# Second batch's keys moved behind the start of the MLP, key sums in four quarters of TensorE, and the last output in two halves

## The chip, the core and the metric

The program runs on one core of a Trainium2 chip. The metric is the device time of one execution in microseconds, as a median of several runs. The engines are TensorE (PE in the profile, its weight loads PEld), VectorE (DVE), ScalarE (ACT), GpSimd (POOL) and SyncE (SP), whose queue issues all DMAs before the change.

## The reference

The program computes a linear attention with a quadratic feature map, and behind it a gated MLP on the attention's output. There are 4 batches, 4 heads, 1088 positions, head size 32, and r = 8.

```python
def phi(x):
    a = np.einsum('rd,bhsd->bhsr', S1, x)
    b = np.einsum('rd,bhsd->bhsr', S2, x)
    return np.einsum('bhsi,bhsj->bhsij', a, b).reshape(*x.shape[:-1], r * r)
q_p, k_p = (phi(q), phi(k))
kv = np.einsum('bhsf,bhsd->bhfd', k_p, v)
z = np.sum(k_p, axis=2)
num = np.einsum('bhsf,bhfd->bhsd', q_p, kv)
den = np.einsum('bhsf,bhf->bhs', q_p, z)[..., None] + 1e-06
attn = num / den
# x = attn as 4352 tokens x 128
xn = x / sqrt(mean(x * x) + 1e-06) * rms_g
g, val = xn @ w_gate, xn @ w_val           # 128 -> 1536
out = (g / (1 + exp(-g)) * val) @ w_out    # 1536 -> 128
```

z is a sum over positions of products a_i b_j. It is therefore the diagonal blocks (one per head) of A^T B, where A holds the 32 columns a of the four heads and B the 32 columns b.

## The kernel before

The 4352 tokens are worked through in chunks of 512 (the ninth has 256). A **slot** is one block of 128 of the 1536 hidden units for one chunk: three MLP products into `g_ps`, three into `v_ps` (L822: each fp32 operand is split in a high and a low fp32r part), a Silu on ACT (L829), a product h on DVE (L833), a split of h (ACT L242; DVE L250 or POOL L249), and three products into `o_ps` (L853), or one plain fp32 product in the first 12 and the last 2 slots (L840). The first two chunks take hidden blocks 0 to 5 first (`CUT`), then blocks 6 to 11; the others take 12 slots in a row. In the first two slots the products are made in halves of 256 tokens (`HEAD`).

The weights arrive as 64-bit words (L383) and are turned into fp32 in five steps (`to_f32`: ACT or DVE L330/L306, then DVE L310, L315, L320, L324), and then split (`split`: ACT L242, POOL L249), 384 columns a hidden block.

Ahead of the MLP's first slot stands the **head** of the program: the keys of batch 0 (`kside(0)`: products with S in L482, the outer product phi on DVE or POOL in L501, kv and z in L531), the queries of chunk 0 (`qphi`: L572, L581, turned in L591), numerator and denominator (`nmm`, L659), the division (DVE L722, L723, L715), the mean square (L729, L739), its root on POOL (L757), the normalised x (L760, L780), its turn on TensorE (L764) and the split in `x_hi` (ACT L787) and `x_lo` (DVE L767). For chunk 0 the division and all after it are done in two halves of 256 tokens.

The keys of batches 1 to 3 go through `kside` and `kv_turned`: `mms` makes 18 products of 64x64 (L482), ACT copies the results (L509), DVE multiplies (L501). In `kvmm` nine products of all 64 columns (a and b of four heads) with the 32 columns b (L401) make a Gram matrix whose blocks hold z, and 36 products (L407) make kv in the four column quarters of the array, one head each. `turn` (L430, L433) spreads and turns the results into `kvs[b]`.

The order of work is written by a planner (`Plan.run`). Each task has a key (the slot by which it is due), a duration in ns for each engine it may run on, and buffers; the planner simulates the engines with these durations and picks tasks by key. Every engine then runs its instructions strictly in the planned order. Where TensorE would idle before 20 us, the planner puts in filler products on zeros (`keep_warm`, L292). The last constants that bear on the change: `K1` are the keys of batch 1's steps and of its loads, `AHEAD` gives batch 1's keys two of the three `att` buffers right behind chunk 0's numerators, `SBD` names batches whose phi is computed from the SBUF copy alone, and `DLAT` is the planner's DMA latency.

Of the kernel before, what the change touches and what calls it, by code (L numbers as in the profile page):

```python
# [10 lines left out]
F32 = mybir.dt.float32  # L11
# [9 lines left out]
R = 8  # L21
# [53 lines left out]
K1 = -41,9,10,-26.5  # L75
SBD = (1,)
AB2 = (-21, -20, -19)
# [3 lines left out]
AHEAD = 1  # L81
DLAT = 2400
# [30 lines left out]
class Plan:  # L113
# [49 lines left out]
    def run(self, clock, filler, slow, urgent, window):  # L163
        clock, todo, out, port, form = dict(clock), self.tasks, [], 0, False
        while todo:
# [33 lines left out]
            t.on, t.end = e, at + ns + (DLAT if e == "dma" else 0)  # L199
# [10 lines left out]
def attention_then_glu(ctx, tc, kT, v, qT, sw, w, gain, out):  # L210
# [25 lines left out]
    def load(nbytes, key, emit, writes, reads=()):  # L236
        plan.add({"dma": (nbytes / 320, emit, 0)}, key, reads, writes)
# [23 lines left out]
    spread = const.tile([NB, H, F], F32, name="spread")  # L261
    for h in range(H):
        nc.vector.tensor_copy(
            out=spread[:, h].rearrange("p (i j) -> p i j", j=R),
            in_=ident[:NB, 2 * h * R:(2 * h + 1) * R].unsqueeze(2).to_broadcast([NB, R, R]),
        )
    column = const.tile([P, R], F32, name="column")
    nc.vector.tensor_reduce(out=column, in_=ident.rearrange("p (o j) -> p j o", j=R), axis=AX.X, op=ALU.add)
# [95 lines left out]
    load(-400 * 320, -99, lambda: nc.sync.dma_start(out=s_raw.rearrange("p n c -> p (n c)"), in_=sw.bitcast(U32)), ["s_raw"])  # L364
# [25 lines left out]
    abs_of, ahead = {}, {}  # L390

    def kv_turned(b, kv, vt, phis, abs_, key):
        acc, tr = ps("att", 3), ps("att", 3)
        both, gram, picked = sb("kv_both", [P, 2, F], 1), sb("gram", [NB, H * R], 1), sb("picked", [P, 2, R], 1)

        def kvmm():
            for t in range(KT):
                ab = abs_[t // 3]()[:, t % 3]  # L400
                nc.tensor.matmul(  # L401
                    out=tr()[:NB, :H * R], lhsT=ab.rearrange("p h c r -> p (h c r)"), rhs=ab[:, :, 1, :], start=(t == 0), stop=(t == KT - 1)
                )
# [9 lines left out]
            1450, key, kvmm, [(phis[g], g) for g in range(3)] + [(vt, g) for g in range(3)] + [(abs_[g], g) for g in range(3)],  # L413
            [acc, tr], True,
        )
        act(H * R, key, lambda: nc.scalar.copy(out=gram(), in_=tr()[:NB, :H * R]), [tr], [gram])
# [10 lines left out]
        def turn():  # L427
            for h in range(H):
# [9 lines left out]
                out=picked(), in0=sums(), in1=column.unsqueeze(1).to_broadcast([P, 2, R]), op=ALU.mult  # L438
# [18 lines left out]
    def kside(b, keys, early):  # L457
# [34 lines left out]
        for i, (lo, hi) in enumerate(groups):  # L492
# [15 lines left out]
            def bring(ab=ab, ab_ps=ab_ps, ts=ts, m=m, o=o, c0=int(first and near)):  # L508
                nc.scalar.copy(  # L509
                    out=ab()[:, ts].rearrange("p t h c r -> p (t h) c r")[:, :, c0:],  # L510
                    in_=ab_ps()[:, o:o + m * HALF].rearrange("p (th c r) -> p th c r", c=2, r=R)[:, :, c0:],
                )
# [4 lines left out]
            if near or b in SBD:  # L517
                dve(m * 268, kphi, lambda outer=outer: outer(nc.vector), [(ab, i), ab_ps] if near else [(ab, i)], [(phi, i)], b in SBD)
# [6 lines left out]
        for i, (lo, hi) in enumerate(groups):  # L525
# [10 lines left out]
            pe(275 * (hi - lo), key, kvmm, [(phis[i], i), (vt, piece[i])], [acc], True)  # L536
# [10 lines left out]
    xs, phiqs = {}, {}  # L547
# [134 lines left out]
    def qside(c, keys, also=None):  # L682
# [9 lines left out]
        if first and AHEAD:  # L692

            ahead[1] = [ps("att", 3) for _ in range(2)]
            if AHEAD > 1:
                abs_of[2] = ps("att", 3)
# [269 lines left out]
```

## Time and profile before

| what | value |
|---|---|
| median of 3 runs | 270.78 us (270.42 to 270.82) |
| the profiled execution's own time | 270.91 us |
| its span, first to last instruction | 269.1 us |
| PE busy | 262.6 us, 98% of the span |
| DVE busy | 189.5 us, 70% |
| ACT busy | 153.2 us, 57% |
| POOL busy | 66.7 us, 25% |
| first MLP product (L822) begins | 19.46 us |
| last output DMA is issued | 266.43 us |

How to read it: the share of busy time is an average over the head, the long MLP stretch and the tail. The granted TensorE clock is shown apart; half of it doubles the time of a product. In the view of the chain of waits, "issue" is time in which an engine waited for nothing that the profile shows. One fp32 product is recorded as two instructions, so 18 products are shown as x36.

### The profile page before, as it was taken

What the parts mean: (1) busy time and instruction counts of PE and PEld (TensorE: products, weight loads), DVE (VectorE), ACT (ScalarE), POOL (GpSimd) and SP (SyncE); (2) the same over time, 40 slices, a digit from 0 to 9 for tenths busy, and PEclk for the clock granted to TensorE, in tenths of its full rate; (3) what the DMA queues carried; (4) which work ended last, traced back from release to release, by engine and by line L of the source; (5) the groups of instructions that cost most, each with busy time, mean ns of one, the idle gap of its engine ahead of it and who ended that gap; (6) DMA issues with size and microseconds to landing.
All of it is one profiled execution on the core that took longest, in us unless ns stands there. A gap on an engine that the chain in (4) does not pass through costs nothing.

```text
span 269.1 us, 5080 instructions
## 1 busy us (share of the span) xinstructions
PE 262.6 (98%) x1899; PEld 208.9 (78%) x1899; DVE 189.5 (70%) x378; ACT 153.2 (57%) x319; POOL 66.7 (25%) x79
## 2 busy tenths in 40 slices
PE   8889999999999999999999999999999999999995
PEld 5758677677887878878887887788887888788894
DVE  5769999666847887677666795678568566766532
ACT  4457763675654544565556554565655565665662
POOL 3033751367350130001800220003300700100262
PEclk9979999999999999999999999999999999999999
DMA  6999500642521520035002500024002200100010
GB/s 202 363 388 371 181 2 0 200 110 58 130 67 48 153 57 2 1 100 131 26 0 80 148 11 2 0 85 130 4 0 68 61 0 0 40 2 0 0 41 21
DMA packets 12953, 22.11 MB, mean 82 GB/s; under 512 B 1664, under 2 KB 5760, under 8 KB 12928
## 3 DMA queue, kind: packets, MB, share of 16 engines
q1 hardware_dynamic: 12928, 21.78, 25.8%
q8 instruction: 15, 0.25, 0.4%
q14 instruction: 10, 0.08, 0.1%
HBM read 18.69 MB, written 3.08 MB: 81 GB/s over the span
## 4 chain that ended last, share of the span: by engine, by line
PE 96%; DMA 2%; issue 1%; SPq 0%; DVE 0%; ACT 0%
PE g_ps L822 27%; PE v_ps L822 27%; PE o_ps L853 23%; PE o_ps L840 4%; PE att L659 4%; DMA q<-qT 2%; PE att L764 2%; PE att L482 2%; PE att L401 1%; PE att L407 1%; PE att L675 1%; PE o_ps L531 1%; PE att L572 1%; PE att L292 1%; PE att L591 0%
## 5 line engine op out<-in xcount | busy, mean ns | idle before, releaser
L833 DVE TENSOR_TENSOR h<-v_ps,s 128x512 f32<-128x512 f32 (+2 forms) x109 | 71.1, 654 | 28.1 <-PE v_ps L822 12.1
L242 ACT CAST h_hi<-h 128x512 fp32r<-128x512 f32 (+1 forms) x91 | 54.2, 596 | 52.5 <-DVE h L833 52.3
L829 ACT ACTIVATE s<-g_ps 128x512 f32<-128x512 f32 (+1 forms) x108 | 62.0, 574 | 25.1 <-PE g_ps L822 22.5
L250 DVE TENSOR_TENSOR h_lo<-h,h_hi 128x512 fp32r<-128x512 f32 x74 | 53.0, 720 | 32.0 <-ACT h_hi L242 31.0
L822 PE MATMUL g_ps<-x_hi,w_hi 128*128 128x512 f32 (+1 forms) x110 | 46.0, 419 | 0.0
L822 PE MATMUL v_ps<-x_hi,w_hi 128*128 128x512 f32 (+1 forms) x110 | 42.2, 383 | 0.0
L822 PE MATMUL g_ps<-x_hi,w_lo 128*128 128x512 f32 (+1 forms) x110 | 42.0, 382 | 0.0
L822 PE MATMUL g_ps<-x_lo,w_hi 128*128 128x512 f32 (+1 forms) x110 | 41.7, 379 | 0.0
L822 PE MATMUL v_ps<-x_hi,w_lo 128*128 128x512 f32 (+1 forms) x110 | 41.5, 377 | 0.0
L822 PE MATMUL v_ps<-x_lo,w_hi 128*128 128x512 f32 (+1 forms) x110 | 41.4, 377 | 0.0
L757 POOL TENSOR_TENSOR rstd<-ms,mhalf 128x4 f32<-128x4 f32 (+1 forms) x10 | 9.5, 951 | 112.3 <-DVE ms L773 111.9
L853 PE MATMUL o_ps<-h_hi,w_lo 128*128 128x512 f32 (+1 forms) x94 | 36.1, 384 | 0.0
L853 PE MATMUL o_ps<-h_hi,w_hi 128*128 128x512 f32 (+1 forms) x94 | 36.1, 384 | 0.0
L853 PE MATMUL o_ps<-h_lo,w_hi 128*128 128x512 f32 (+1 forms) x94 | 36.0, 383 | 0.0
L249 POOL TENSOR_TENSOR h_lo<-h,h_hi 128x512 fp32r<-128x512 f32 (+1 forms) x20 | 20.4, 1029 | 30.7 <-ACT h_hi L242 30.6
L822 PEld LDWEIGHTS g_ps<-x_hi,w_hi 128*128 128x128 f32 x110 | 20.7, 188 | 6.5 <-issue 1.8
L822 PEld LDWEIGHTS g_ps<-x_hi,w_lo 128*128 128x128 f32 x110 | 20.7, 188 | 5.0 <-issue 1.7
L822 PEld LDWEIGHTS v_ps<-x_hi,w_hi 128*128 128x128 f32 x110 | 20.7, 188 | 4.6 <-DVE ms L773 0.2
L249 POOL TENSOR_TENSOR w_lo<-w_f,w_hi 128x256 fp32r<-128x256 f32 (+1 forms) x24 | 17.2, 734 | 28.2 <-ACT w_hi L242 28.1
L822 PEld LDWEIGHTS g_ps<-x_lo,w_hi 128*128 128x128 f32 x110 | 20.9, 190 | 4.2
L822 PEld LDWEIGHTS v_ps<-x_hi,w_lo 128*128 128x128 f32 x110 | 20.7, 188 | 4.1 <-issue 0.2
L822 PEld LDWEIGHTS v_ps<-x_lo,w_hi 128*128 128x128 f32 x110 | 20.6, 188 | 4.0
(104 smaller groups left out, 301.3 us busy)
## 6 DMA issues: line engine op xcount, KB each, us to landing
w_raw<-w SPq DMA_DIRECT2D x12, 384.0 KB
at<-far SPq DMA_DIRECT2D x12, 256.0 KB
bt<-far SPq DMA_DIRECT2D x24, 128.0 KB
q<-qT SPq DMA_DIRECT2D x8, 256.0 KB
outT<-o_sb SPq DMA_DIRECT2D x8, 256.0 KB
vt<-v SPq DMA_DIRECT2D x9, 204.0 KB
kt<-kT SPq DMA_DIRECT2D x9, 192.0 KB
far<-abt SPq DMA_DIRECT2D x12, 64.0 KB
```

The source lines that it names most:

```text
L242: "act": (n * 0.835 + 172, lambda: nc.scalar.copy(out=out(), in_=in_()), 0),
L249: "pool": (n * 2.1 + 150, lambda: nc.gpsimd.tensor_tensor(out=out(), in0=in_(), in1=hi(), op=ALU.subtract), 0),
L250: "dve": (n * 1.04 + 140, lambda: nc.vector.tensor_tensor(out=out(), in0=in_(), in1=hi(), op=ALU.subtract), penalty, True),
L482: nc.tensor.matmul(out=abv[hf * HALF:(hf + 1) * HALF, t - t0, :], lhsT=kt()[:, s0:s0 + HALF], rhs=sblk_t, start=True, stop=True)
L659: nc.tensor.matmul(out=nv[hf * HALF:(hf + 1) * HALF, t, p, :], lhsT=phiqs[c][1]()[:, p, l0:l0 + HALF], rhs=kvs[(STARTS[c] + l0) // S][:, p ...
L757: nc.gpsimd.tensor_tensor(out=rstd()[:, us, 0], in0=ms()[:, us], in1=mhalf[:, us], op=ALU.pow)
L764: nc.tensor.transpose(out=xt()[:, t * P:(t + 1) * P], in_=xn()[:, t, :], identity=ident)
L822: nc.tensor.matmul(out=acc()[:, cs], lhsT=wt[:, j, i3, :], rhs=x()[:, cs], start=(i == 0), stop=(i == 2))
L829: act(n, t + 0.3, lambda: nc.scalar.activation(out=s()[:, :n], in_=gps()[:, :n], func=AF.Silu), cols(gps, whole[0]), [s])
L833: lambda cs=cs: nc.vector.tensor_tensor(out=h()[:, cs], in0=vps()[:, cs], in1=s()[:, cs], op=ALU.mult),
L840: lambda cs=cs: nc.tensor.matmul(out=o_ps()[:, cs], lhsT=w_f[:, j, 2], rhs=h()[:, cs], start=first, stop=last and cs.stop == n),
L853: nc.tensor.matmul(out=o_ps()[:, :n], lhsT=wt[:, j, 2, :], rhs=x()[:, :n], start=first and i == 0, stop=last and i == 2,)
```

## The change

It has three named parts and some constants of the planner.

1. **z in four quarters.** In `kvmm` product t no longer multiplies 64 columns by 32, but the 32 columns a by the 32 columns b, and writes into rows 32 (t mod 4) to 32 (t mod 4) + 31 of the same bank; so each column quarter of the array gets two or three of the nine products. The Gram matrix then has 128 rows (four partial sums), `gram` is 128x32, and `spread` has 128 rows, so that L430's products add the quarters. The copy `ab` is laid out so that the 32 columns a are adjacent. `spread` and `column` are now made by POOL (`patterns`, six instructions) where DVE had made them with five.
2. **Batch 1's keys.** `K1` changes, `AHEAD` and `SBD` go: the 18 products L482 of batch 1 stand behind chunk 1's turn and no longer between chunk 0's numerators and its turn. Their phi reads one operand from PSUM, as batches 2 and 3 do.
3. **Last output.** The last chunk's two halves of 128 columns go to two tiles of their own (`o_end0` by ACT, `o_end1` by DVE), and each has a DMA of its own, on ACT's queue and on SP's.

The planner's DMA rate goes from 320 to 340 bytes a ns, its DMA latency from 2400 to 1900 ns, POOL's start from 2200 to 5200 ns, and three durations of TensorE tasks are lowered. The keys of chunk 2's first query steps return to the general rule.

```diff
-K1 = -41,9,10,-26.5
-SBD = (1,)
-AB2 = (-21, -20, -19)
+K1 = (8, 9, 10, -9)
-AHEAD = 1
-DLAT = 2400
...
-        plan.add({"dma": (nbytes / 320, emit, 0)}, key, reads, writes)
+        plan.add({"dma": (nbytes / 340, emit, 0)}, key, reads, writes)
...
+    spread = const.tile([P, H, F], F32, name="spread")
+    column = const.tile([P, 4 * R], F32, name="column")
+    def patterns():
+        nc.gpsimd.tensor_tensor(out=column, in0=ident[:, :4 * R], in1=ident[:, 4 * R:8 * R], op=ALU.add)
+        for k in (2, 3):
+            nc.gpsimd.tensor_tensor(out=column, in0=column, in1=ident[:, 4 * k * R:4 * (k + 1) * R], op=ALU.add)
+        nc.gpsimd.tensor_copy(
+            out=spread.rearrange("p h (i j) -> p (h i) j", j=R), in_=column.unsqueeze(2).to_broadcast([P, H * R, R])
+        )
+        for k in (2, 1):
+            nc.gpsimd.tensor_tensor(out=column[:, :k * R], in0=column[:, :k * R], in1=column[:, k * R:2 * k * R], op=ALU.add)
...
         def kvmm():
             for t in range(KT):
-                ab = abs_[t // 3]()[:, t % 3]
-                nc.tensor.matmul(
-                    out=tr()[:NB, :H * R], lhsT=ab.rearrange("p h c r -> p (h c r)"), rhs=ab[:, :, 1, :], start=(t == 0), stop=(t == KT - 1)
-                )
+                a, b = (abs_[t // 3]()[:, c, t % 3].rearrange("p h r -> p (h r)") for c in range(2))
+                rows = slice(t % 4 * H * R, (t % 4 + 1) * H * R)
+                nc.tensor.matmul(out=tr()[rows, :H * R], lhsT=a, rhs=b, start=(t < 4), stop=(t >= KT - 4), skip_group_check=True)
...
-            near = i not in FAR if first else b in NEAR and b not in SBD
+            near = i not in FAR if first else b in NEAR
...
+        if not left:
+            for i, cs in enumerate(rest_of):
+                o_end, wd = sb(f"o_end{i}", [P, P], 1), cs.stop - cs.start
+                if i:
+                    dve(wd * 1.04, t + 1.0, lambda cs=cs, o=o_end: nc.vector.tensor_copy(out=o(), in_=o_ps()[:, cs]), done, [o_end])
+                else:
+                    act(wd, t + 1.0, lambda cs=cs, o=o_end: nc.scalar.copy(out=o(), in_=o_ps()[:, cs]), done, [o_end])
+                load(
+                    wd * P * 4, t, lambda cs=cs, o=o_end, on=nc.sync if i else nc.scalar: on.dma_start(
+                        out=out[:, s0 + cs.start:s0 + cs.stop], in_=o()
+                    ), [("out", c, i)], [o_end],
+                )
+            return
...
-    plan.run({"pe": PE0, "act": 1900, "dve": 1000, "pool": 2200, "dma": 600}, keep_warm, SLOW, URGENT, WINDOW)
+    plan.run({"pe": PE0, "act": 1900, "dve": 1000, "pool": 5200, "dma": 600}, keep_warm, SLOW, URGENT, WINDOW)
```

The planner's new order shows at three places. First TensorE between chunk 0's numerators and the first MLP products, before (L659 are the numerators, L482 batch 1's keys, L292 filler, L764 the turn of one half of x, L572 chunk 1's queries, L822 the MLP):

```order
L659 MATMUL att<-kv_82,phiq 64x66 x16
L482 MATMUL att<-s_t,kt 64x64 x18
L292 MATMUL att<-const-float32-0.0 1x128 x2
L764 MATMUL att<-ident,xn 128x128 x2
L292 MATMUL att<-const-float32-0.0 1x128 x2
L764 MATMUL att<-ident,xn 128x128 x2
L572 MATMUL att<-s_t,q 128x64 x2
L822 MATMUL g_ps<-x_hi,w_hi 128x256
```

And now (L295 is filler, L757 the turn, L815 the MLP):

```order
L659 MATMUL att<-kv_83,phiq 64x66 x16
L295 MATMUL att<-const-float32-0.0 1x128 x9
L757 MATMUL att<-ident,xn 128x128 x2
L295 MATMUL att<-const-float32-0.0 1x128 x2
L815 MATMUL g_ps<-x_hi,w_hi 128x256
L815 MATMUL g_ps<-x_hi,w_lo 128x256
L815 MATMUL g_ps<-x_lo,w_hi 128x256
L815 MATMUL v_ps<-x_hi,w_hi 128x256
L815 MATMUL v_ps<-x_hi,w_lo 128x256
L815 MATMUL v_ps<-x_lo,w_hi 128x256
```

Nine fillers stand where the keys stood, and nine half-width MLP products (the six shown and three more into `g_ps`) now go ahead of the second turn and of chunk 1's queries.

Second DVE from the first query outer product of chunk 0 (`phn`) to the first division, before:

```order
L581 TENSOR_TENSOR phn<-att,abq 128x512 x2
L605 COPY phiq<-g_ps 128x2x256
L310 TENSOR_SCALAR w_tmp<-w_tmp 128x384
L540 COPY kv_82<-o_ps 64x2x33
L315 TENSOR_SCALAR w_tmp<-w_tmp 128x384
L320 SCALAR_TENSOR_TENSOR w_tmp<-w_raw,w_tmp 128x384
L324 SCALAR_TENSOR_TENSOR w_f<-w_raw,w_tmp 128x384
L722 TENSOR_SCALAR den<-att 128x8
L723 RECIPROCAL rden<-den 128x8
L715 TENSOR_TENSOR x<-att,rden 128x256
```

And now:

```order
L581 TENSOR_TENSOR phn<-att,abq 128x512 x2
L313 TENSOR_SCALAR w_tmp<-w_tmp 128x384
L318 TENSOR_SCALAR w_tmp<-w_tmp 128x384
L323 SCALAR_TENSOR_TENSOR w_tmp<-w_raw,w_tmp 128x384
L327 SCALAR_TENSOR_TENSOR w_f<-w_raw,w_tmp 128x384
L309 TENSOR_SCALAR w_tmp<-w_raw 128x384
L313 TENSOR_SCALAR w_tmp<-w_tmp 128x384
L715 TENSOR_SCALAR den<-att 128x8
L716 RECIPROCAL rden<-den 128x8
L708 TENSOR_TENSOR x<-att,rden 128x256
```

The copies of `phiq` and `kv` left DVE (both are ACT's now), and two steps of the second hidden block's weights (L309, L313) came in ahead of the division.

Third TensorE at the start of chunk 1's MLP, before (L840 is the plain fp32 product into `o_ps`, L764 the turn of chunk 1's x):

```order
L840 MATMUL o_ps<-h,w_f 128x512 x3
L764 MATMUL att<-ident,xn 128x128 x4
L822 MATMUL g_ps<-x_hi,w_hi 128x512
L822 MATMUL g_ps<-x_hi,w_lo 128x512
L822 MATMUL g_ps<-x_lo,w_hi 128x512
L822 MATMUL v_ps<-x_hi,w_hi 128x512
```

And now (L833 is that product, L757 the turn):

```order
L833 MATMUL o_ps<-h,w_f 128x512 x2
L757 MATMUL att<-ident,xn 128x128 x4
L833 MATMUL o_ps<-h,w_f 128x512
L482 MATMUL att<-s_t,kt 64x64 x18
L815 MATMUL g_ps<-x_hi,w_hi 128x512
L815 MATMUL g_ps<-x_hi,w_lo 128x512
L815 MATMUL g_ps<-x_lo,w_hi 128x512
```

Batch 1's 18 products stand behind chunk 1's turn. Chunk 0's sixth hidden block, which followed the turn before, is made ahead of it now. Everywhere behind this place TensorE has the same products as before in nearly the same order, the Gram products with 32 columns in place of 64.

More of the change, by code (lines that the diff above doesn't have):

```diff
@@ L259, in attention_then_glu @@
     nc.vector.memset(ones, 1.0)
[L261 to L265, printed above, removed]
-        )
-    column = const.tile([P, R], F32, name="column")
-    nc.vector.tensor_reduce(out=column, in_=ident.rearrange("p (o j) -> p j o", j=R), axis=AX.X, op=ALU.add)
+    spread = const.tile([P, H, F], F32, name="spread")
[6 more added lines that the diff above has]
+            out=spread.rearrange("p h (i j) -> p (h i) j", j=R), in_=column.unsqueeze(2).to_broadcast([P, H * R, R])
+        )
+        for k in (2, 1):
+            nc.gpsimd.tensor_tensor(out=column[:, :k * R], in0=column[:, :k * R], in1=column[:, k * R:2 * k * R], op=ALU.add)
+    patterns()
     zeros = nc.const_aps.tensor(0.0, [P, P], F32)
@@ L412, in kv_turned @@
         pe(
-            1450, key, kvmm, [(phis[g], g) for g in range(3)] + [(vt, g) for g in range(3)] + [(abs_[g], g) for g in range(3)],
+            1330, key, kvmm, [(phis[g], g) for g in range(3)] + [(vt, g) for g in range(3)] + [(abs_[g], g) for g in range(3)],
             [acc, tr], True,
         )
-        act(H * R, key, lambda: nc.scalar.copy(out=gram(), in_=tr()[:NB, :H * R]), [tr], [gram])
+        act(H * R, key, lambda: nc.scalar.copy(out=gram(), in_=tr()[:, :H * R]), [tr], [gram])
         act(
@@ L437, in kv_turned @@
             17, key, lambda: nc.vector.tensor_tensor(
-                out=picked(), in0=sums(), in1=column.unsqueeze(1).to_broadcast([P, 2, R]), op=ALU.mult
+                out=picked(), in0=sums(), in1=column[:, :R].unsqueeze(1).to_broadcast([P, 2, R]), op=ALU.mult
             ), [tr], [picked],
@@ L472, in kside @@
         piece = [next(g for g, (_, e) in enumerate(pieces) if hi <= e) for _, hi in groups]
-        abs_ = [sb("ab", [P, 3, H, 2, R], 3) for _ in groups]
+        abs_ = [sb("ab", [P, 2, 3, H, R], 3) for _ in groups]
         phis = [sb("phi", [P, 3, H * F], 4) for _ in groups]
-        banks = [ps(("g_ps", "v_ps")[i % 2], 2) for i in range(4)] if first else ahead[b] if b in ahead else [ps("att", 3) for _ in range(2)]
+        banks = [ps(("g_ps", "v_ps")[i % 2], 2) for i in range(4)] if first else [ps("att", 3) for _ in range(2)]
         def mm(lo, hi, ab_ps, t0):
@@ L667, in abmm @@
         q, m = phiqs[c][0], CHUNKS[c] // 2
-        if c not in abs_of:
-            abs_of[c] = ps("att", 3)
-        ab_ps = abs_of[c]
+        ab_ps = abs_of[c] = ps("att", 3)
         def emit():
@@ L691, in qside @@
         nums = {u: ps("att", 3) for u in range(0, nt, 2)}
[L692 to L696, printed above, removed]
         if c >= NATURAL:
@@ L873, in slot @@
         else:
-            for i, cs in enumerate(rest_of):
-                if i:
-                    dve(
-                        (cs.stop - cs.start) * 1.04, t + 1.0,
-                        lambda cs=cs: nc.vector.tensor_copy(out=o_sb()[:, cs], in_=o_ps()[:, cs]), done, cols(o_sb, cs),
-                    )
-                else:
-                    act(cs.stop - cs.start, t + 1.0, lambda cs=cs: nc.scalar.copy(out=o_sb()[:, cs], in_=o_ps()[:, cs]), done, cols(o_sb, cs))
+            act(n, t + 1.0, lambda: nc.scalar.copy(out=o_sb()[:, :n], in_=o_ps()[:, :n]), done, cols(o_sb, whole[0]))
         load(n * P * 4, t, lambda: nc.sync.dma_start(out=out[:, s0:s0 + n], in_=o_sb()[:, :n]), [("out", c)], cols(o_sb, whole[0]))
```

27 lines of the change are left out of this document (13 added, 14 removed).

## The prediction

> **What bounds the kernel now.** I read the page first: busy shares and the chain that ended last.
>
> ```profile
> span 269.1 us, 5080 instructions
> PE 262.6 (98%) x1899; PEld 208.9 (78%) x1899; DVE 189.5 (70%) x378; ACT 153.2 (57%) x319; POOL 66.7 (25%) x79
> PE 96%; DMA 2%; issue 1%; SPq 0%; DVE 0%; ACT 0%
> ```
>
> TensorE is the bound, in share and in chain. Then its waits over the whole span (line, releaser, total us, times, longest):
>
> ```profile
> PE att L482 <- issue: 1.2, 1, 1.2
> PE att L292 <- PEq L959: 0.8, 1, 0.8
> PE att L572 <- DMA q<-qT: 0.6, 1, 0.6
> PE att L482 <- PE att L482: 0.6, 1, 0.6
> ```
>
> There are four waits of note, and all belong to the head. Two stand before or in batch 1's keys. From the first MLP product to the last, TensorE waits for nobody, so there a product added or removed counts in full. Only the head and the tail have slack. The chain of waits in order of time shows the head (start, us, what):
>
> ```profile
> 11.39 1.35 PE att L659 x32
> 12.74 1.17 issue
> 13.92 0.93 PE att L482 x24
> ...
> 16.13 0.94 PE att L292 x4
> 17.07 0.62 PE att L764 x2
> 19.65 0.41 PE g_ps L822 x3
> 23.64 0.59 PE att L591 x4
> ```
>
> Behind chunk 0's numerators TensorE has idle time; batch 1's 18 products (36 records) fill part of it. They cost the stream nothing there, but they and the two fillers behind them end at 17.07, and only then does the first turn of x (L764) get its place. The other engines show that x was ready sooner:
>
> ```profile
> 9.22 0.56 ACT L330 ACTIVATE w_tmp<-w_raw 128x384 f32<-128x384 f32 x1 [1.14 <-DMA w_raw<-w]
> 10.59 0.35 DVE L310 TENSOR_SCALAR w_tmp<-w_tmp 128x384 f32<-128x384 f32 x1
> 12.36 0.56 DVE L324 SCALAR_TENSOR_TENSOR w_f<-w_raw,w_tmp 128x384 uint32<-128x384 uint32 x1
> 12.95 0.17 DVE L722 TENSOR_SCALAR den<-att 128x8 f32<-128x8 f32 x1
> 15.49 0.42 DVE L760 TENSOR_TENSOR xn<-x,rstd 128x256 f32<-128x256 f32 x1
> 17.73 0.47 ACT L787 ACTIVATE x_hi<-att,gain_t 128x256 fp32r<-128x256 f32 x1 [1.06 <-PE att L764]
> 18.10 0.68 ACT L780 ACTIVATE xn<-x,rstd 128x128 f32<-128x128 f32 x2
> 18.24 0.48 DVE L767 SCALAR_TENSOR_TENSOR x_lo<-att,gain_t,x_hi 128x256 fp32r<-128x256 f32 x1 [1.75 <-ACT x_hi L787]
> 19.82 0.41 ACT L242 CAST w_hi<-w_f 128x256 fp32r<-128x256 f32 x1
> 22.83 0.68 DVE L581 TENSOR_TENSOR phn<-att,abq 128x512 f32<-128x512 f32 x1
> ```
>
> The first normalised half was finished at 15.91 and lay for 1.1 us; DVE idled 1.75 us for the result of its turn. Last the clock, in stretches cut where the granted clock changes (us, busy PE, PEld, DVE, ACT, POOL, then PEclk):
>
> ```profile
> 5.42:8.83 3.41, 2.84 (x64) 2.64 (x66) 3.25 (x5) 1.14 (x5) 1.07 (x1) 1.00 0.95 330
> 12.24:15.66 3.42, 1.66 (x49) 1.44 (x47) 3.18 (x14) 1.68 (x7) 1.44 (x2) 1.00 1.03 386
> 15.66:19.07 3.41, 3.41 (x23) 1.67 (x19) 1.50 (x5) 2.07 (x9) 1.17 (x2) 0.50 1.02 384
> ```
>
> A stretch in which TensorE was busy 1.66 of 3.42 us is followed by one at half clock; one with 2.84 of 3.41 is not.
>
> **Part 1, z in quarters.** Batch 1's sums and kv in the chain:
>
> ```profile
> 44.31 1.17 PE att L401 x18
> 45.47 1.14 PE att L407 x72
> ```
>
> Nine Gram products (18 records) take 1.17 us, 65 ns a record, though they stream only 32 columns. The 36 kv products in four quarters take 1.14/72 = 16 ns a record, a quarter of that, though they stream 64. So a record costs some 65 ns on its own strip of the array, and four strips run side by side. The new Gram products have the kv products' form: 32 columns of weights, four quarters in turn, one bank. By that row they take 18 x 16 ns = 0.29 us and save 0.88 us; three batches save 2.64 us. Nothing covers these products, so the saving is whole. Bounds: the 18 keys products of another batch, in two halves (first row below), take 1.20/36 = 33 ns a record, which would be 0.60 us and 1.7 us saved in all; with no overlap nothing is saved. A loss is excluded: the weights have half the columns, the moving side is the same. I take the kv row, the nearest in every respect.
>
> The Trainium skill, "TensorE: Matmul & The Clock Gate", section "Wait — 56ns, not 53.3ns?", says that matmuls never start closer than about 25 ns, however small. By it 18 records would need 0.45 us, the three batches would save 2.15 us, and the sum below would be an estimated 0.5 us smaller. The kv row, 16 ns, goes under that floor, so the measurement decides here.
>
> The gram copy on ACT and the spread products (L430) keep their column counts; their 128 rows for 64 cost nothing that is counted by columns. `spread` and `column` go to POOL at the start. POOL's next work there stands in this row:
>
> ```profile
> 5.80 1.07 POOL L501 TENSOR_TENSOR phi<-ab 128x512 f32<-128x512 f32 x1 [3.89 <-ACT ab L509]
> ```
>
> It idled 3.89 us before it. Six small instructions, none over the 1.07 us of this 128x512 one and most a sixteenth of its size, fit in: 0, at worst 0.3 us if they slow DVE's first conversion.
>
> **Part 2, the keys.** What 18 such products cost inside the stream is seen at batch 2:
>
> ```profile
> 94.77 1.20 PE att L482 x36
> 95.97 0.89 PE g_ps L822 x3
> 96.86 0.70 PE v_ps L822 x3
> ```
>
> 1.20 us, and the next three MLP products take 0.89 where three take 0.70: 1.39 us added. On DVE the three outer products stay behind chunk 1's turn, where they were; the three ACT copies come in there, under a TensorE that has its products queued. Between the turn of chunk 1 and its first product there are now one `o_ps` product and these keys, which cover `x_hi` and `x_lo`; with no cover there would be a wait.
>
> Against this stands the head. DVE begins the first weights when ACT's step ends (9.22 + 0.56 = 9.78), no longer waits for the copy of `phiq`, and has six steps ahead of the division: four of 0.35 and two of 0.56, so den comes at about 12.35 where it stood at 12.95. The second weights' data must have landed by 11.6 for that; before, ACT took them at 11.9 only because it was busy. xn stood 2.54 us behind den and lasted 0.42: 15.3 for its end. Nine fillers (0.94/4 = 0.24 us a record at half clock, half that at full: 2.1 us in all) are done by 14.9. So the turn goes at 15.35, not 17.07. `x_hi` follows at 15.8 to 16.3; DVE does two steps of 0.56 first, then `x_lo` until 16.95. MLP products begin at 16.3, in earnest at 16.95, where they began at 19.65.
>
> That is not yet the gain, for the second turn and chunk 1's queries now fall behind this start. I compare at L591 before 23.64, ahead of which the same products stand, now with one more block of three, 0.70 plus some 0.1. It waits for DVE's second `phn`. DVE from 16.95: 1.82 for a weights block (until 18.8), `x_lo` of the second half (whose ACT chain ends at 19.0: 16.3 + 0.41 + 0.56 + 0.68, a turn of 0.4, `x_hi` with a cast 0.65) until 19.5, then `phn` twice 0.69, four steps of 0.35 and two of 0.56: 23.4, or 23.2 with the overlaps of some 0.08 between neighbours that the rows show. 0.4 us earlier and 0.8 us of work ahead: 1.2 us gained. Bounds: nothing, if the lead is eaten, and 1.7 us, the shift of the turn. I take 1.2.
>
> **Part 3, the end.**
>
> ```profile
> 264.73 1.04 PE L840 MATMUL o_ps<-h,w_f 128*128 128x256 f32 x6
> 265.81 0.27 ACT L881 COPY o_sb<-o_ps 128x128 f32<-128x128 f32 x1 [1.34 <-PE o_ps L840]
> 266.11 0.29 DVE L878 COPY o_sb<-o_ps 128x128 f32<-128x128 f32 x1 [1.06 <-ACT o_sb L881]
> 266.43 0.33 SPq L882 DMA_DIRECT2D outT<-o_sb  x1
> ```
>
> DVE's copy waited for ACT's, since both wrote one tile. With two tiles it starts with it: 0.30 us. The DMA on ACT's queue is issued beside SP's, so it costs nothing unless it is slower than SP's; no row shows one. Half the bytes each may save a little more. I take 0.3, between 0 and 0.6.
>
> **Sum.** -2.64 + 1.39 - 1.2 - 0.3 = -2.75 us, against the profiled execution's 270.91 (1.8 us of it lie outside its span of 269.1): 268.16. That execution is 0.13 us over the median of 270.78, so 268.1 stands for the median.
>
> **Rivals.** (a) *Half clock again.* With nine fillers TensorE is busy about 2.9 (0.5 of numerators, 2.1 of fillers, 0.3 of a turn) in the 3.42 us that had 1.66, which by the two rows above should hold the clock. If it falls none the less, the first MLP products and the turns run at half rate until 19.07, and the second `x_lo` comes 0.8 us later: the head gains 0.4, the time is 268.9. The Trainium skill, same page, "What's actually happening", says that the window runs freely and does not start with the kernel; so another execution may be cut otherwise. One trace cannot show that. Chance 0.15.
>
> (b) *Quarters at the rate of halves,* because three products in one quarter follow each other and the group is short: 1.7 saved for 2.64, 269.0. For: halves are what L482 and L659 show. Against: L407. Chance 0.1. That quarters do not overlap at all, and the change thus does not do what it says, gives 268.1 + 2.64 = 270.7, no change; 0.04.
>
> (c) *Weights late, slower than before.* The MLP starts earlier, and the sixth hidden block now stands ahead of chunk 1's turn; DVE and POOL must have it ready. The rows:
>
> ```profile
> 24.00:28.00 4.00, 4.00 (x44) 2.69 (x42) 4.00 (x14) 2.97 (x9) 0.99 (x2) 1.00 1.00 351
> 31.79 2.20 POOL L249 TENSOR_TENSOR w_lo<-w_f,w_hi 128x256 fp32r<-128x256 f32 x3
> L833 DVE TENSOR_TENSOR h<-v_ps,s 128x512 f32<-128x512 f32 (+2 forms) x109 | 71.1, 654 | 28.1 <-PE v_ps L822 12.1
> ```
>
> DVE is full there, and before, this block's low part was done at 32.5 behind the root of chunk 1. TensorE will now ask for it at 31.2. Were it as late as before, the wait would be 1.3 us and the time 269.4; it makes the kernel slower from 34.0 on, and at 34.6 the time is 271.5. Against it: this root now follows the block in POOL's order, the keys' loads no longer precede the weights, and DVE's idle 1.75 us is used. From 23.2 DVE has until that block's last step three products h of 0.65, four weight steps of 0.56, two of 0.35, a division's 0.42 and four small ones of some 0.2: 6.1 us, so 29.3; ACT's cast of 0.41 and POOL's part, a third of 2.20, make it 30.4. Chance 0.07 for slower, 0.06 for the milder wait.
>
> **How the numbers follow.** The forecast's own case, 267.3 to 268.8, has 0.55; gains still larger, 0.03. A measurement here tells 0.2% (0.54 us) from no change. Faster than 270.2: the forecast and larger gains 0.58, (a) 0.15, (b) 0.10, the milder (c) 0.06, together 0.89, less 0.03 for an unnamed loss: 0.86. Same: 0.04 and 0.02 of these, 0.06. Slower: 0.07 and 0.01, 0.08. The range, 267.1 to 269.9, takes in (a), (b) and the milder (c); 0.18 stay outside.
>
> **What would show it.** Quarters: the 18 Gram records in about 0.3 us at three places. Keys: 36 records of L482 at about 35 us, with 1.2 us. Head: the first turn at about 15.4, the first MLP product at about 16.3, PEclk at 1.00 in the stretch behind. Weights: no wait of TensorE between 20 and 45 us. End: the two last copies starting together, the last issue 1.4 us, not 1.7, behind the begin of TensorE's last six records. I am wrong if the Gram records take over 0.6 us, or if TensorE waits more than 1 us in all behind 20 us.

## The result and the profile after

| | forecast | measured |
|---|---|---|
| median of 4 runs | 268.1 us (267.1 to 269.9) | 268.75 us (268.26 to 269.0) |
| kernel before, beside it | 270.78 us | 270.6 us |
| ratio to before | 0.990 | 0.9931, 95% interval 0.9912 to 0.995 |
| profiled execution | 268.16 us from 270.91 | 269.00 us, span 267.2 us |

The change is faster by 0.7%, on the side forecast and inside the range, but by two thirds of the size. The page of the changed kernel answers to the three rows quoted of before:

```profile
span 267.2 us, 5106 instructions
PE 261.3 (98%) x1913; PEld 206.6 (77%) x1913; DVE 190.4 (71%) x371; ACT 155.3 (58%) x327; POOL 64.3 (24%) x82
PE 85%; DMA 5%; DVE 4%; SPq 2%; issue 1%; ACT 0%; POOL 0%; POOLq 0%
```

TensorE is still the bound, but the chain that ended last is no longer 96% its own: DMA and DVE now stand in it for 9%. That is the first sign that something other than TensorE's own work sets places of the stream. The chain in order of time shows the keys (L482) in their new place and the sums at two batches (start, us, what):

```profile
36.37 1.20 PE att L482 x36
37.57 0.89 PE g_ps L815 x3
38.46 0.70 PE v_ps L815 x3
...
45.06 0.27 PE att L403 x17
45.34 1.04 PE att L407 x70
...
101.41 0.27 PE att L403 x17
101.68 1.04 PE att L407 x70
```

The keys cost 1.20 + 0.89 - 0.70 = 1.39 us, to the hundredth what batch 2 had shown. Gram and kv together took 1.17 + 1.14 = 2.31 us a batch and now take 1.31: 1.0 us saved where 0.88 was forecast. The timeline of the head (start, duration, engine, line):

```profile
9.84 0.55 ACT L333 ACTIVATE w_tmp<-w_raw 128x384 f32<-128x384 f32 x1 [2.00 <-DMA w_raw<-w]
12.95 0.16 DVE L715 TENSOR_SCALAR den<-att 128x8 f32<-128x8 f32 x1
15.86 0.41 PE L757 MATMUL att<-ident,xn 128*128 128x128 f32 x2 [0.78 <-DVE xn L753]
23.63 0.55 PE L591 MATMUL att<-ident,phn 128*128 128x128 f32 x3 [0.45 <-DVE phn L581]
```

Here the forecast had 9.22, 12.35, 15.35 and 23.2: everything is 0.4 to 0.6 us late, from the first weights on. The clock, in the stretches cut as before, did not fall:

```profile
12.24:15.66 3.42, 2.84 (x38) 1.98 (x34) 3.22 (x16) 1.43 (x7) 1.57 (x2) 1.00 1.03 408
15.66:19.07 3.41, 3.16 (x21) 2.26 (x21) 3.30 (x8) 2.53 (x10) 2.36 (x3) 1.00 0.99 331
```

TensorE was busy 2.84 us (forecast 2.9) in the stretch that had 1.66, and the next was granted in full. A place that the forecast did not have stands far behind the head. The chain passes there through a DMA and POOL:

```profile
69.08 5.50 DMA bt<-far
74.59 0.03 POOLq L641
74.62 0.36 POOL h_lo L245
75.02 0.50 PE o_ps L846
```

POOL waited for `bt`, made `phiq` of it (L641), and only then split h; TensorE's product with `h_lo` came at 75.02. The timeline gives the product ahead of it 74.32, and neighbours 0.23 apart: 0.47 us lost. The end, at last:

```profile
264.15 0.27 ACT L866 COPY o_end<-o_ps 128x128 f32<-128x128 f32 x1 [1.18 <-PE o_ps L833]
264.45 0.37 ACTq L868 DMA_DIRECT2D outT<-o_end  x1
264.45 0.29 DVE L864 COPY o_end<-o_ps 128x128 f32<-128x128 f32 x1 [0.90 <-ACT o_end L866]
264.77 0.33 SPq L868 DMA_DIRECT2D outT<-o_end  x1
```

DVE's copy still waits for ACT's, although each has a tile of its own.

### The profile page after: what moved, and what is told of

Its sections match the earlier page's. It is cut to its first block, busy times and chain, and to the rows that moved or that the text cites. A ratio compares the mean times of both kernels' runs of the same rounds, so it can differ in the third digit from the quotient of the medians.

```text
span 267.2 us, 5106 instructions
## 1 busy us (share of the span) xinstructions
PE 261.3 (98%) x1913; PEld 206.6 (77%) x1913; DVE 190.4 (71%) x371; ACT 155.3 (58%) x327; POOL 64.3 (24%) x82
## 4 chain that ended last, share of the span: by engine, by line
PE 85%; DMA 5%; DVE 4%; SPq 2%; issue 1%; ACT 0%; POOL 0%; POOLq 0%
PE g_ps L815 25%; PE v_ps L815 25%; PE o_ps L846 22%; PE o_ps L833 4%; PE att L659 3%; DMA w_raw<-w 2%; DMA bt<-far 2%; PE att L482 1%; PE att L757 1%; PE att L407 1%; PE att L673 1%; DMA far<-abt 1%; SPq L635 1%; DVE w_tmp L313 1%; DVE w_tmp L318 1%
## 5 line engine op out<-in xcount | busy, mean ns | idle before, releaser
L238 ACT CAST h_hi<-h 128x512 fp32r<-128x512 f32 (+1 forms) x94 | 56.1, 596 | 53.6 <-DVE h L826 53.1
L246 DVE TENSOR_TENSOR h_lo<-h,h_hi 128x512 fp32r<-128x512 f32 x77 | 56.6, 738 | 37.7 <-ACT h_hi L238 36.9
L822 ACT ACTIVATE s<-g_ps 128x512 f32<-128x512 f32 (+1 forms) x108 | 62.0, 574 | 27.2 <-PE g_ps L815 25.5
L815 PE MATMUL g_ps<-x_hi,w_hi 128*128 128x512 f32 (+1 forms) x110 | 46.3, 421 | 0.0
L815 PE MATMUL g_ps<-x_hi,w_lo 128*128 128x512 f32 (+1 forms) x110 | 42.1, 382 | 0.0
L815 PE MATMUL v_ps<-x_hi,w_hi 128*128 128x512 f32 (+1 forms) x110 | 41.9, 381 | 0.0
L815 PE MATMUL g_ps<-x_lo,w_hi 128*128 128x512 f32 (+1 forms) x110 | 41.7, 380 | 0.2 <-DVE x_lo L760 0.2
L815 PE MATMUL v_ps<-x_hi,w_lo 128*128 128x512 f32 (+1 forms) x110 | 41.5, 377 | 0.0
L815 PE MATMUL v_ps<-x_lo,w_hi 128*128 128x512 f32 (+1 forms) x110 | 41.5, 377 | 0.0
L245 POOL TENSOR_TENSOR h_lo<-h,h_hi 128x256 fp32r<-128x256 f32 (+1 forms) x17 | 16.5, 980 | 41.0 <-ACT h_hi L238 40.8
L815 PEld LDWEIGHTS g_ps<-x_hi,w_hi 128*128 128x128 f32 x110 | 20.6, 188 | 7.0 <-issue 1.6
L641 POOL TENSOR_TENSOR phiq<-at,bt 128x512 f32<-128x512 f32 (+1 forms) x14 | 18.6, 1333 | 26.4 <-DMA bt<-far 26.4
L815 PEld LDWEIGHTS g_ps<-x_hi,w_lo 128*128 128x128 f32 x110 | 20.7, 188 | 5.4 <-issue 1.7
L815 PEld LDWEIGHTS g_ps<-x_lo,w_hi 128*128 128x128 f32 x110 | 20.9, 190 | 4.7 <-DVE x_lo L760 0.6
L815 PEld LDWEIGHTS v_ps<-x_hi,w_hi 128*128 128x128 f32 x110 | 20.7, 188 | 4.4
L815 PEld LDWEIGHTS v_ps<-x_lo,w_hi 128*128 128x128 f32 x110 | 20.7, 188 | 4.0
L815 PEld LDWEIGHTS v_ps<-x_hi,w_lo 128*128 128x128 f32 x110 | 20.7, 188 | 3.9
```

The lines of the kernel that those rows point to most:

```text
L238: "act": (n * 0.835 + 172, lambda: nc.scalar.copy(out=out(), in_=in_()), 0),
L245: "pool": (n * 2.1 + 150, lambda: nc.gpsimd.tensor_tensor(out=out(), in0=in_(), in1=hi(), op=ALU.subtract), 0),
L246: "dve": (n * 1.04 + 140, lambda: nc.vector.tensor_tensor(out=out(), in0=in_(), in1=hi(), op=ALU.subtract), penalty, True),
L641: eng.tensor_tensor(out=phi()[:, p, :n], in0=at()[:, p, :n], in1=bt()[:, p, :n], op=ALU.mult)
L815: nc.tensor.matmul(out=acc()[:, cs], lhsT=wt[:, j, i3, :], rhs=x()[:, cs], start=(i == 0), stop=(i == 2))
L822: act(n, t + 0.3, lambda: nc.scalar.activation(out=s()[:, :n], in_=gps()[:, :n], func=AF.Silu), cols(gps, whole[0]), [s])
```

## The experiments

| label | what differs | median us | ratio to before (95%) |
|---|---|---|---|
| e1 | before + quarters | 267.04 | 0.9879 (0.9849 to 0.9908) |
| e2 | e1 + last output in halves | 267.07 | 0.988 (0.9851 to 0.9909) |
| e9 | e1 + keys moved | 268.06 | 0.9914 (0.9887 to 0.994) |
| e5 | e2 + keys moved | 269.34 | 0.9967 (0.9951 to 0.9984) |
| e3 | change, keys in the head | 268.37 | 0.9935 (0.9912 to 0.9958) |
| e7 | the change again | 268.49 | 0.9928 (0.9905 to 0.9951) |
| e12 | change, DMA constants as before | 268.19 | 0.9902 (0.9871 to 0.9934) |
| e10 | change, early loads | 268.83 | 0.9939 (0.9916 to 0.9962) |
| e6 | change, patterns on DVE | 268.58 | 0.9928 (0.9906 to 0.995) |
| e11 | change, no fillers | 269.91 | 0.9995 (0.9969 to 1.0021) |
| e8 | change, second bank at the end | 271.53 | 1.0049 (1.0029 to 1.0069) |
| e4 | change, one, two and four strips | 268.81 (one run) | |

The rows come from four chips: e1 to e4 from one, e5 to e8, e9 to e11 and e12 from one each. The kernel before had medians of 270.01, 270.15, 270.31 and 270.55 us beside them, so between rows of different chips a difference of under some 0.5 us tells little by itself.

### The quarters alone (e1), and with the new end (e2)

e1 is the kernel before with the first part alone (the sum pattern made by one DVE reduction); e2 adds the third part to it:

```diff
-                    out=tr()[:NB, :H * R], lhsT=ab.rearrange("p h c r -> p (h c r)"), rhs=ab[:, :, 1, :], start=(t == 0), stop=(t == KT - 1)
+                rows = slice(t % 4 * H * R, (t % 4 + 1) * H * R)
+                nc.tensor.matmul(out=tr()[rows, :H * R], lhsT=a, rhs=b, start=(t < 4), stop=(t >= KT - 4), skip_group_check=True)
```

> The kernel before with the Gram products in four quarters and nothing else: same order of work, batch 1's keys in the head, one last output, patterns made by VectorE. If the quarters save what the two traces show (Gram and kv together 1.31 us for 2.31), three batches give 3.0 us: about 267.6 us, faster than the whole change (268.75). Rival, by the predicted 0.88 us each: 268.0. Rival, that the change's gain came from its new order and the quarters only shift work to the next wait: no less than 269.5.

> The same with the last output in two halves as the change has it. The stretch from TensorE's last product to the end of the span was 3.33 us before and 3.11 with the change; so 0.2 us under the quarters alone, 267.4 us. Rival, that the second queue costs as much at the end as it saves: no difference.

Both take 267.05 us, 3.0 us less than the 270.01 of before beside them, and 1.4 to 1.7 us less than the whole change. So the quarters are the whole gain: 1.0 us a batch, as the chain above has it, in three batches. The new end is worth nothing that the times tell, though e2's trace has 3.11 us from TensorE's end to the span's, e1's 3.32. These two beat both kernels.

### One, two and four strips (e4)

The change, with the Gram products of batch 1 in one strip of 32 columns, of batch 2 in two, of batch 3 in four:

```diff
-                rows = slice(t % 4 * H * R, (t % 4 + 1) * H * R)
+                k = {1: 1, 2: 2, 3: 4}[b]
+                rows = slice(t % k * H * R, (t % k + 1) * H * R)
```

> The change with the Gram products of batch 1 in one quarter, of batch 2 in two, of batch 3 in four (the sums are the same). If a record costs some 65 ns on its own strip and strips run side by side, the 18 records take about 1.2, 0.6 and 0.3 us. Rival, the cost goes by columns of weights (32 for 64): 0.6 us in all three. Rival, a floor of 25 ns from one record to the next: 0.45 us in the third.

The chain at the three batches:

```profile
44.08 0.65 PE att L404 x17
44.73 1.04 PE att L408 x70
...
100.53 0.40 PE att L404 x17
...
159.40 0.27 PE att L404 x17
```

From two strips to one the piece grows by 0.25 us, from four to two by 0.13: strips do run side by side, as forecast. But one strip alone takes 0.65 where the old form took 1.17. From the first of these records to the first kv record behind them the timeline has 0.53, 0.28 and 0.15 us for 17 records: 31 ns a record on one strip, 16 on two, 9 on four. The step "a record costs some 65 ns on its own strip" therefore fell: halving the weight columns from 64 to 32 halved it. Four shapes fit one rule, about 1 ns for each column of the wider side, weights or stream, in each part of the array that works beside the others: 65 ns at 64 and 32 (before's L401), 4 x 16 at 32 and 64 (L407), 2 x 33 at 64 and 64 (L482), 31 at 32 and 32. The two sides were not varied one at a time beyond these rows.

### Keys and planner constants (e3, e9, e5)

e3 is the change with the second part undone and the other new constants kept; e9 and e5 move the keys and keep the old constants, e9 with the old end, e5 with the new one. e9's and e5's TensorE order is the same.

```diff
-K1 = -41,9,10,-26.5
-SBD = (1,)
-AHEAD = 1
+K1 = 8, 9, 10, -9
+SBD = ()
+AHEAD = 0
```

> The change with its second part undone: batch 1's keys in the head, by the kernel before's keys, two buffers ahead and phi from the copy; the planner's new rates, POOL's patterns, quarters and end stay. If moving the keys costs 1.39 us in the stream and gives back 0.63 us in the head, undoing it gains 0.76 us, and 0.77 us of waits for POOL may go or stay: 267.2 to 268.0. Rival, by the prediction (head 1.2 us): 268.5. If the planner's rates and POOL's patterns cost something of their own, it stays above the quarters and end alone by that.

> Quarters and end as in the run of both (267.07 us, 0.988 of before), and batch 1's keys behind chunk 1's turn with phi from PSUM; planner rates and VectorE's patterns stay as before. In the stream the keys cost 1.39 us; the head now has eleven fillers where they stood, and by the order both turns stand ahead of the first MLP product as before. If the head gives back 0.63 us as in the change, 267.8 us. If, as the run with the keys in the head says, the move is free by itself, 267.1 us. If the head gives nothing back, 268.4 us.

> The kernel before with the quarters and with batch 1's keys behind chunk 1's turn (the planner's other constants as before), and the last output as before: one DMA, on SP's queue. e5 had the same order of TensorE's work with the two halves at the end; its TensorE ended only 0.56 us later than e2's, but its last issue on ACT's queue took 2.40 us where e2's took 0.38, and its time was 269.34. Theory A: the keys cost 0.5 to 0.8 us and the rest of e5's time was that one issue; then this kernel takes 267.5 to 267.9 us (ratio about 0.991), TensorE's last product ends 3.3 us before the span's end. Theory B: the long issue belonged to the profiled execution alone and the keys cost 2.3 us; then this kernel takes about 269.3 us.

With the old constants the move costs 268.06 - 267.04 = 1.0 us (e9, e1): theory A's mechanism, at a price somewhat over its 0.5 to 0.8. The two medians are from two chips; the traces agree with the size, for batch 1's first Gram record stands at 43.62 us in e2 and at 44.71 in e9. e5's further 1.3 us lies behind TensorE's last product: TensorE ends at 262.7 us in e5 and at 263.1 in e9, and the spans end 5.0 and 3.3 us later. e5's timeline and the DMA queues of its last microseconds (queue, kind: packets, MB, share):

```profile
263.11 2.40 ACTq L874 DMA_DIRECT2D outT<-o_end  x1
263.38 0.33 SPq L874 DMA_DIRECT2D outT<-o_end  x1
```

```profile
q14 instruction: 1, 0.01, 0.9%
```

ACT's issue took 2.40 us, 0.37 in the change, and a packet on an instruction queue falls beside it, which e2's last microseconds do not have. All eleven runs of e5 (268.96 and up) lie above all four of e9 (up to 268.55), so it is no accident of one execution. What the issue waited for is not shown: e9 and e12 have such a packet too, at about 262.6 us, ahead of their last issues, which took 0.33 and 0.56 us.

e3's 268.37 against e2's 267.07 says that the new constants and POOL's patterns, with the keys where they were, cost 1.3 us. By the starts of its products, e3's TensorE lost 0.9 us at 26 and 27 us to POOL's `w_lo` and DVE's `h`, where e2's lost nothing. Against e3 the move would cost only 0.1 to 0.4 us (268.49 and 268.75 for the change), near the forecast's 0.2; but e3 carries these waits, which the change does not have, so e9 against e1 is the cleaner price.

### The change again, patterns on DVE, early loads (e7, e6, e10)

e7 has no edit. e6 gives `spread` and `column` back to DVE. e10 puts batch 1's loads where they were:

```diff
-K1 = (8, 9, 10, -9)
+K1 = (8, 9, 10, -26.5)
```

> The change itself again beside these, for a comparison on one chip: 0.993 of before, some 268.1 to 268.7 us.

> The whole change, but spread and column made by VectorE; the order of all other work is the change's. In the change's trace one step of the first conversion took 0.84 us beside POOL's memsets where it took 0.20 us before, and the converted S was done at 4.32 us for 3.71. If that delay reaches the MLP, up to 0.6 us under the change itself; if the first keys' DMA (4.3 us) covers it, no difference.

> The change, but with the loads of batch 1's keys issued right behind the second hidden block's weights, as before; the planner moves the steps behind them. Theory A (what delays the head is the transfers queued behind the first weights): ACT begins the first weights at 9.2 to 9.3 us and not at 9.84, den comes at 12.3 to 12.6, the first MLP product 0.3 to 0.6 us sooner than 16.84, and the time is 268.0 to 268.3 us. Theory B (the queue behind does not matter): ACT begins at 9.8 as in the change and the time is the change's, 268.5 to 268.8.

The patterns' engine does not matter. e10's head came as theory A had it (first weights 9.29, den 12.39, first MLP product 16.29), but its time is theory B's, and e7, with the change's own loads, had nearly the same head:

```profile
12.46 0.16 DVE L715 TENSOR_SCALAR den<-att 128x8 f32<-128x8 f32 x1
15.38 0.41 PE L757 MATMUL att<-ident,xn 128*128 128x128 f32 x2 [0.75 <-DVE xn L753]
16.36 0.39 PE L815 MATMUL g_ps<-x_hi,w_hi 128*128 128x256 f32 x1
17.12 0.78 DVE L318 TENSOR_SCALAR w_tmp<-w_tmp 128x384 uint32<-128x384 uint32 x1
23.15 0.66 PE L591 MATMUL att<-ident,phn 128*128 128x128 f32 x4 [0.44 <-DVE phn L581]
```

These are the forecast's 12.35, 15.35, 16.3 and 23.2. So the queue behind the first weights is not what delayed the head of the first profile: one program begins its weights at 9.36 in one execution and at 9.84 in another. The step DVE L318 takes 0.78 where its neighbours take 0.35; TensorE waits 0.4 us at 23.15 for the end of that row of steps. e10 brings its second L591 to 22.44 us and then loses the lead: by the starts, TensorE waits 0.9 us for POOL's `w_lo` and DVE's `h` at 25 and 26 us, and 0.5 for `h_lo` at 75.

### No fillers (e11)

The change without the eleven fillers around the first turn.

```diff
-    plan.run({"pe": PE0, "act": 1900, "dve": 1000, "pool": 5200, "dma": 600}, keep_warm, SLOW, URGENT, WINDOW)
+    plan.run({"pe": PE0, "act": 1900, "dve": 1000, "pool": 5200, "dma": 600}, lambda k: (lambda: None), SLOW, URGENT, WINDOW)
```

> The change without the eleven filler products around the first turn of x; no result depends on them. Theory A (the fillers hold the clock): TensorE is busy only some 0.7 to 1.0 us of the stretch from about 12.2 to 15.7, the next stretch of 3.4 us shows a granted clock of 0.50, the products in it take twice as long, and the time grows by 0.4 to 1.0 us over the change's 268.5, to 268.9 to 269.5. Theory B (the fillers do nothing): no stretch at 0.50, or it costs nothing, and the time is 268.3 to 268.7.

```profile
8.83:12.24 3.41, 3.41 (x73) 2.79 (x69) 2.29 (x7) 2.50 (x7) 0.00 (x0) 1.00 1.01 390
12.24:15.66 3.42, 0.59 (x10) 0.36 (x6) 3.25 (x16) 1.31 (x6) 1.57 (x2) 0.91 1.03 408
15.66:19.07 3.41, 2.85 (x13) 2.55 (x12) 3.01 (x7) 2.01 (x6) 2.26 (x3) 0.50 1.05 391
19.07:22.48 3.41, 3.41 (x21) 3.41 (x20) 3.04 (x7) 2.29 (x7) 1.28 (x2) 0.59 0.73 227
```

With 0.59 of 3.42 us busy, nearly two stretches follow at half clock, and the time is 1.2 to 1.4 us above the change's, more than theory A's 0.4 to 1.0. All ten executions show it: a mean granted clock of 0.986 to 0.994, against 0.999 to 1.0 in all ten of the change (its first four and e7's).

The profiled execution, 272.23 us, is the slowest of the ten, and not by the clock alone: behind 60 us its TensorE also waits some 2.5 us for POOL, by the starts. The dip's own price stands ahead of that. From the numerators (11.08 us) to batch 1's first Gram record (45.98) pass 34.90 us, where e7 has 33.35: 1.55 us, near the difference of the medians.

The executions of the kernel before divide in the same way. Of the 57 listed beside these runs, 36 have a mean clock of at least 0.998 and a median of 270.0 us; 16 have 0.994 or less and a median of 270.9. The profiled one, 270.91 at 0.992, is of the second kind: its stretch at 0.50 is not in most executions. Nor does the busy time of the stretch ahead of it decide. e2 has the order of before in the head, was busy 1.64 us there, and kept its clock:

```profile
12.24:15.66 3.42, 1.64 (x44) 1.43 (x46) 3.18 (x14) 1.56 (x5) 1.45 (x2) 1.00 1.04 371
15.66:19.07 3.41, 3.09 (x30) 2.00 (x30) 2.22 (x7) 2.67 (x11) 1.16 (x2) 1.00 1.03 393
```

e1, with the same order, was busy 1.65 us and was granted 0.53 in the next stretch.

### A second bank for the last half (e8)

The change, with the last chunk's second 128 columns accumulated in a PSUM bank of their own, so that its products are 128 columns wide:

```diff
-                    out=o_ps()[:, :n], lhsT=wt[:, j, 2, :], rhs=x()[:, :n],
+                    for cs, bk, os in outs:
+                        out=bk()[:, os], lhsT=wt[:, j, 2, :], rhs=x()[:, cs],
```

> The change, with the last chunk's second half of 128 columns summed in a PSUM bank of its own, so that its products are issued as two of 128 columns for one of 256, 11 slots long. If the two last copies run one behind the other only because they read one bank (VectorE waits for ScalarE by the program), they now start together, and the stretch from TensorE's last product to the end of the span falls from 3.1 to 2.8 us. The halved products may cost up to 0.4 us ahead of it. If the copies still run one after the other, something else orders them.

```profile
258.03 0.28 PE L817 MATMUL v_ps<-x_lo,w_hi 128*128 128x256 f32 x1
...
258.32 0.27 PE L849 MATMUL o_ps<-h_hi,w_lo 128*128 128x128 f32 x1
258.43 0.28 PE L849 MATMUL att<-h_hi,w_lo 128*128 128x128 f32 x1
...
266.81 0.29 DVE L867 COPY o_end<-att 128x128 f32<-128x128 f32 x1 [0.90 <-PE att L835]
```

DVE's copy now waits for TensorE and not for ACT: what ordered the copies was that both read one PSUM tile in one bank, not that they wrote one output tile. e8 gives the second half another tile and another bank at once, so it does not tell the two apart. TensorE's end to the span's end shrinks from 3.11 to 2.81 us, the 0.3 that the third part was forecast to bring. But a product of 128 columns is followed by the next after 0.11 us, one of 256 after 0.12, so each split product costs nearly double. The forecast allowed up to 0.4 us for that; the median is 3.0 us above e7's, on the same chip, and 0.5% above before.

### The planner's DMA constants (e12)

```diff
-        plan.add({"dma": (nbytes / 340, emit, 0)}, key, reads, writes)
+        plan.add({"dma": (nbytes / 320, emit, 0)}, key, reads, writes)
-            t.on, t.end = e, at + ns + (1900 if e == "dma" else 0)
+            t.on, t.end = e, at + ns + (2400 if e == "dma" else 0)
```

> The change with two of the planner's constants as before: DMA latency 2400 ns and rate 320 bytes a ns, where the change has 1900 and 340. With them the planner puts POOL's first split of h at about 72 us ahead of the query product phiq again, whose operand bt arrives by DMA; in the change phiq stands first, waits for that DMA until 72.4 us, and the split behind it comes late. Theory A (this order makes TensorE's waits for h_lo, which the change has at 74.32 us, 0.47, and another execution at 73.94 and 99.38, 0.19 and 0.38): no wait for POOL's h_lo between 50 and 135 us, the way from the end of batch 1's kv to the end of batch 2's first Gram records is 54.2 to 54.4 us as in the runs without that order (54.8 and 55.1 in the change), and the time is 267.7 to 268.2 us. Theory B (the waits come from elsewhere or move): the way stays at 54.7 to 55.1 us and the time at 268.4 to 268.8.

POOL in the change, and in e12:

```profile
72.41 1.29 POOL L641 TENSOR_TENSOR phiq<-at,bt 128x512 f32<-128x512 f32 x1 [4.22 <-DMA bt<-far]
73.66 2.56 POOL L245 TENSOR_TENSOR h_lo<-h,h_hi 128x512 fp32r<-128x512 f32 x2
```

```profile
71.84 1.31 POOL L245 TENSOR_TENSOR h_lo<-h,h_hi 128x512 fp32r<-128x512 f32 x1 [3.53 <-ACT h_hi L238]
74.31 1.30 POOL L641 TENSOR_TENSOR phiq<-at,bt 128x512 f32<-128x512 f32 x1 [1.16 <-DMA bt<-far]
```

The planner that takes DMA for faster puts `phiq` first, and POOL stands 4.22 us before a transfer with a split of h behind it. With the old constants the split goes first, no wait of TensorE for `h_lo` is left behind 50 us, and from batch 1's first Gram record to batch 2's pass 55.81 us, 0.5 and 0.8 less than in the two profiles of the change (56.35 and 56.60), as theory A said. The time, 268.19 us, is 0.3 to 0.6 us under the change's medians. The intervals of the ratios overlap, and four of the change's ten executions lie in e12's range, so the size rests on the traces, which agree with it. They also show that the order alone does not make the wait: e6's profile has `phiq` first too (71.65), yet no such wait in its view (0.15 us by the starts, at 129), and 55.91 us between the same records. What is lost differs from execution to execution.

## Why the prediction was right or wrong

The side was right, and for its first reason: the quarters. A ledger from 270.0 us, the median of the kernel before at full clock, each line from the run named:

| step | forecast, from 270.91 | measured, from 270.0 | from |
|---|---|---|---|
| quarters | -2.64 | -3.0 | e1, e2: 267.05 |
| keys in the stream | +1.39 | +1.39 | the change's chain |
| head | -1.2 | -0.4 | e9: 268.06 |
| end | -0.3 | 0 | e2 against e1 |
| POOL's order | none | +0.3 to +0.6 | e12 against the change |
| sum | 268.16 | 268.3 to 268.6 | measured 268.49 and 268.75 |

The head's and POOL's lines are differences of these same medians, so the sum must come out near the measured times; what is open in it is the 0.13 us between e9 and e12. That the forecast came within 0.4 to 0.7 us is partly luck. The quarters saved 0.4 us more than forecast and the base was 0.9 lower; against that the head saved 0.8 less, the end 0.3 less, and POOL's order was not in the sum.

**Quarters.** Strips side by side: right (e4). "A record costs some 65 ns on its own strip": wrong for 32 columns of weights; the 18 records took about 0.18 us, not 0.29, and kv products begin among the last of them. The floor of 25 ns that the page "TensorE: Matmul & The Clock Gate" of the Trainium skill gives, section "Wait — 56ns, not 53.3ns?", does not hold across four strips: 9 ns a record here.

**Keys.** Right to the hundredth. But the part as a whole is a loss of 1.0 us by e9 and e1, and not of 0.2, because of the head.

**Head.** Every time in it was met by e7's profile to some 0.1 us: den, first turn, first MLP product, second `phn` turn at 23.15; the change's first profile has them 0.4 to 0.6 later. The failing step is "I compare at L591 before 23.64". That row came from an execution with 3.4 us at half clock, which most executions of before do not have. Here are the first turn of `phn` and the one that the forecast compares in e2, with the keys where they were and the clock at 1.00, and then the first in e7, whose other stands above at 23.15:

```profile
9.40 0.66 PE L590 MATMUL g_ps<-ident,phn 128*128 128x128 f32 x4
22.94 0.66 PE L590 MATMUL att<-ident,phn 128*128 128x128 f32 x4
9.12 0.66 PE L591 MATMUL g_ps<-ident,phn 128*128 128x128 f32 x4
```

e7 has one block of 0.8 us more ahead of the compared turn, began 0.28 us earlier and is there 0.21 us later. That makes 0.8 - 0.28 - 0.21 = 0.3 us gained, not 1.2; e9's time gives 0.4, with a head in which both turns of x still stand ahead of the MLP. "That execution is 0.13 us over the median of 270.78" looked like reassurance, but with three runs the median was no better: the full-clock executions of before lie at 270.0. What the fillers now save is a dip that befell 16 of 57 runs.

**End.** "With two tiles it starts with it" was wrong: the PSUM tile and bank that both read order the copies, not the output tile (e8). The Trainium skill says on the page "PSUM — Partial Sum Buffer", section "PSUM bank collisions raise a hardware error", that two engines must not be in one bank at once, reads included; I had not weighed it, and e8 agrees: with two banks the program no longer makes DVE wait for ACT. The 0.2 us that e2's trace gained over e1's did not show in the times. That the issue on ACT's queue "costs nothing" held in the change (0.37 us) and not in e5 (2.40).

**Not forecast: POOL's order.** I took the planner's DMA rate and latency for constants without a term. They moved `phiq` ahead of a split of h, and a wait took the place of slack. My own sign of being wrong, "TensorE waits more than 1 us in all behind 20 us", was met by a little: the view of waits sums only to 0.7 us, but the starts of the products give 0.6 us at L591 and 0.6 for `h_lo` at two places, in the change's profile and in e7's.

**Rivals.** (a) Half clock: not in the change; e11 shows that the fillers prevent it and that it would cost over 1 us, more than the 0.8 that I gave it. (b) Halves: fell. No overlap: fell. (c) Weights late: TensorE did not wait for the sixth hidden block in the change; e10 and e3 have one wait of 0.3 us in the view for the low part of an earlier block, at 25 and 26 us.

What stays open: why the new constants with the keys in the head (e3) cost 1.3 us was read from its waits only and not tried apart; the slow DVE step (L318) has no cause shown, nor has e5's long issue; and whether the PSUM tile or the bank orders the last copies is not shown.

## What to carry to other kernels

Before a difference is read against a row of one execution, look whether that row lies in a stretch at reduced clock, and whether the other executions have it: the mean granted clock of each run tells. In a planned program, a constant of the planner is an edit to the order of every engine, far from the place where it was tuned: compare the order of all queues, and price what each moved instruction now waits for. Small products can share the array by column strips, and narrowing their weights paid as well (65 to 31 ns a record). And try the parts of a change one by one: here the first alone was 1.4 to 1.7 us faster than the whole.

## What the runs showed of the hardware

- Gram products of 32 by 32 columns follow each other after 31 ns on one strip, 16 on two, 9 on four; the form with 64 columns of weights took 65 in its one place. The Trainium skill's "TensorE: Matmul & The Clock Gate", section "LDWEIGHTS (loading the stationary operand)", makes a weight load proportional to its columns: an estimated 27 ns for 32 and 53 for 64. The runs on one strip agree in direction.
- With TensorE busy 2.84 of 3.4 us the next stretch was granted 1.00; with 1.66 it was 0.50 in the profiled execution of before, with 1.65 0.53 in e1's, with 1.64 1.00 in e2's; with 0.59 it was 0.50 and 0.59 in the next two (e11). That the same program has the dip in some executions only agrees with what the Trainium skill says in "TensorE: Matmul & The Clock Gate", section "What's actually happening": the window runs freely.
- Two engines that read different columns of one PSUM tile, in one bank, are put in turn by the built program: 0.3 us here.
- One DMA issue took 2.40 us in place of 0.37, at one place of one program, with a packet on an instruction queue beside it.
- A 128-column product costs about as much as a 256-column one, when each has a weight load of its own: 0.11 against 0.12 us to the next product (e8).
